# A fused attention and gated convolution kernel: a new written-out order of the same operations, with the 64-row score products in fewer runs

## The chip, the cores and the metric

The kernel runs on one core of one Trainium2 chip. A core has TensorE (PE, matrix products, with its weight loads listed as PEld), VectorE (DVE), ScalarE (ACT), GpSimd (POOL) and SyncE (SP). The engines run on their own and wait for each other through semaphores. The metric is the device time of one execution in microseconds (us), as a median over runs.

## What is computed

The inputs are q, k and v (4 batches, 8 heads, 768 positions, head size 64), a projection, a filter and an output matrix. In short:

```python
scores = q @ k^T / 8 - slope[h] * dist        # kept: the last 96 positions, and the first 8 ("global") ones
a = softmax(scores over the kept positions)
x = (a @ v), heads side by side               # 4 x 768 x 512
x1, x2, x3 = x @ w_proj, split in three
y = x1 * circular_convolution(x2, filter) * x3    # over the 768 positions, by Fourier transforms
out = y @ w_out
```

## The kernel before

Each batch goes through attention, gates and convolution. The work of all four batches is laid out as one list of operations, and one text says in which order every engine does them.

**The list.** `Plan.op` adds an operation: a cost per engine that may do it, what it reads and writes, and the PSUM banks that it takes (`acq`) or empties (`use`). An operation is a small group of instructions of one engine: eight banks of PSUM exist, an operation of TensorE takes one or two of them, and later operations on ACT or DVE copy the result out and so free them.

**The order.** The text `ORDER` holds one word for each operation: its number in the list, the engine that does it (P TensorE, A ACT, V DVE, G POOL, S SP) and, for an operation of TensorE, its banks. `119P45` is operation 119 on TensorE in banks 4 and 5, `120A` operation 120 on ACT. A word such as `i26b1` is 26 idle products into bank 1 (method `busy`, L302), which keep TensorE busy at the start. `Plan.schedule` only reads this text and checks it; the costs are not used in it. Each engine then does its own words in the order of the text, and waits where an operation needs data, or a bank that another engine has still to empty.

**The operations that matter here**, with their lines:

- *scores* (L680; in the first batch with added distance products, L671): q times k for two heads and two or three key tiles. Each product uses 64 of the 128 rows of TensorE, one head in the upper half and one in the lower. An operation has 4 or 6 such products (8 to 18 more with the distances), takes two banks, and is followed by one *exp* on ACT (L694), and but for the first batch by one mask product on DVE (L711). There are 48 score operations: 4 batches, 4 head pairs, 3 groups of key tiles. All other products of the kernel use 128 rows, but for a few of the setup.
- *values* (L729, L734), then *rc* and *xn* on DVE or ACT (the division, L758, L753 or L757), *trx* (a turn of x, L774) and its copy *xT*.
- *gate* (L843): x1 and x3, with their copies *x1* and *x3*, and *g* on DVE (L855).
- *butterfly* on DVE (L788 to L799), *proj* (L910), *fwd* (L614, and L593 for the filter), *prod* and *sums* on DVE, *inv* (L935, L938) with the copy *eo*, *mix* (L1018 to L1022), *half* and *y\*g* (L1041) on DVE, *out* (L962) with the copy *ot*, and the store.
- the turns of q and k (L627, L640) with the copies *qT* and *kT*.
- the filter's own transform in the first batch: sums on DVE (L556 to L572), `fwd` products, and copies.

**The loads.** POOL issues nearly all loads, one after the other, in the order of its words: keys (`kn`) and values (`vn`) by tile, q, blocks of the projection matrix (`w256`, `w0`, `w1280`, `w1024`, `w512`), the filter and `wo`. SP issues the first batch's q, the copies of the 8 global rows of k and v into the other tiles (`kglobal`, `vglobal`), and the stores. POOL also makes the tables of distances (operations 22 and 24) and the identity (operation 5).

Numbers used further on: 59, 61, 54 load key tiles 4, 6, 2 of the first batch; 157, 161, 163 to 169 are turns of k and scores of the first batch; 53 copies the global value rows to five tiles; 101, 106 are xn; 360 turns keys 0 and 1 of the second batch, and 404 is a copy xT; 249 is a product of the filter's transform; 283 is a proj, 400 a values, 410 a gate; 588 and 614 turn keys of the third batch; 973 is the last inv of the last batch, 994 to 1002 are its mix, half and y\*g steps, 1015 its last y\*g, and 1003, 1006, 1009, 1016, 1019, 1022 its last six out.

Of the kernel before, what the change touches and what calls it, by code (L numbers as in the profile page):

```python
# [16 lines left out]
P = 128  # L17
# [28 lines left out]
106V 4V 117P23 118A 167P01 168A 165P67 166A 163P45 164A 99P23 100V 101V 215P0 216A 76A 107P1 108V 130P67 131V  # L46
132V 125P23 126V 127V 217V 218V 169P45 170A 73A 102P1 103A 220P6 360P7 488G 490S 272G 495G 133P2 134A 219A
221A 128P3 129V 176P45 177V 178V 361V 171P01 172V 150P3 152V 173V 222V 223V 140P2 142A 356P4 357A 179P5 180V
135P7 358P3 359A 224A 137A 174P2 175V 209V 226V 201V 202V 151P4 153A 154V 204V 371P01 365P23 366A 372A 145P5
147V 208V 203V 210V 211V 205V 206V 196P4 227P6 232A 146P7 148A 149V 234V 230V 235V 212V 207V 213V 236V 237V  # L50
225V 373V 214V 136P5 138A 198A 182P2 192P3 194A 368P01 369A 362P45 363A 197P7 199A 191P3 141P0 143A 228A 231A
193A 229A 233A 144V 238V 370V 195V 298P1 285P0 286A 281P7 282A 184A 386P6 387A 299A 498G 499G 294P0 295A 384P7
385V 239V 367V 139V 283P3 284A 186P6 188A 394P45 395A 397P01 398A 430P7 431V 289P2 290V 364V 181P3 309P6 310A
183A 432P7 433V 240V 396V 503G 504G 278G 489G 492G 485G 486G 502G 497G 487G 388P45 389A 391P01 392A 434P2 435V
390V 491S 505G 501G 496G 187P6 189A 296P7 297A 379P45 380V 381V 436P23 437A 374P01 375V 399V 376V 393V 720G
247P6 248A 439P45 440A 441V 438V 307P7 308A 287P2 288A 241P3 442P01 443A 405P45 406V 190V 407V 242V 382P6 383A
243P7 244A 302P2 303A 400P01 401V 402V 377P6 378V 444V 445P45 446A 447V 408P7 245P3 246A 300P2 301A 249P01
251A 409A 250V 403P6 404A 253P45 254A 255A 304V 292V 448P23 449V 450A 185V 453P01 454V 291V 455V 293V 252V
200V 311V 312V 722S 493S 729G 426P7 420P6 421P4 415P5 417A 422A 423A 411P0 413A 410P1 584P5 585A 456P6 457V
305V 660P4 661A 588P0 589V 306V 717G 713G 735G 716G 718S 494S 714G 313P2 314A 317P3 451P5 452A 412A 318A 479V  # L60
478V 425P6 614P2 615A 727G 734G 506G 726G 280G 732G 662P0 719S 721S 464P4 466A 428A 427A 586P1 587V 414V 612P5
613V 481V 480V 725G 508G 724G 658P3 730G 500G 715G 728G 731G 733G 723G 507G 736G 321P2 322A 663A 323P4 324A
327P1 328V 429V 482V 659V 424V 483V 474P7 476A 319P2 320A 469P0 471A 599P45 600A 590P67 591A 325P2 315P1 316A
326A 473P0 475V 484V 329V 330V 331V 522P3 523A 625P45 596P67 597A 598V 622P01 623A 624V 468P2 526P3 527A 470A
626A 509P6 510V 592V 332V 333V 524P7 525A 616P01 593P23 594A 617A 511P6 512V 601V 595V 336V 513P7 514A 664P45
665A 619P23 667P01 668A 620A 458P6 460V 477V 337V 459P7 461A 517P4 416P5 418A 518A 607P01 602P23 603V 608V
419V 604V 609V 621V 618V 334V 666V 335V 627V 515P7 516A 535P5 536A 530P6 531A 350P4 351A 537P5 812P7 813A
353P6 354A 673P23 674A 538A 670P01 671A 463P4 465A 528P7 529A 842P6 843V 628P23 629V 462V 630V 675V 672V 344P5
610P6 611A 345A 816P4 890P7 605P2 606A 817A 633P01 634V 635V 669V 520V 539V 519V 533V 472V 347P6 348A 631P5
886P3 636P2 637A 887A 632A 891A 341P4 676P01 677V 814P6 815A 342A 681P23 682V 540V 678V 532V 683V 467V 534V  # L70
521V 840P5 841A 644P7 888P6 889A 646A 648P4 650A 653P5 655A 679P0 680A 643P1 645V 847P67 848A 821P45 822A
684P2 547P0 548V 685V 823V 706V 849V 707V 649P3 651A 555P6 556A 549P7 550A 853P01 827P45 828A 898P23 899A
545P6 546A 854A 338P7 339V 708V 340S 349S 352S 355S 346S 343S 638P4 640A 551P5 552A 541P2 553P3 554V 709V 710V
711V 543P6 544A 542A 557V 558V 712V 559V 702P7 818P01 819A 850P45 851A 687P6 639P3 641A 689A 642V 900V 820V
560V 652V 561V 564V 754P2 755A 704A 741P4 742A 844P01 845A 846V 829V 824P23 825A 826V 565V 562V 901P67 902A
739P5 740A 737P4 738A 750P0 892P23 895P67 896A 893A 751A 686P1 688A 752P5 692P4 694A 753A 763P2 743P3 765P0
766A 835P67 836V 837V 563V 903V 697P4 654P1 656A 764A 767V 894V 852V 897V 745P0 746A 699A 744A 578P5 758P1
756P2 757A 759A 856P67 857V 647V 855V 696P4 698A 566P3 567A 579A 568S 580S 830P01 831V 832A 858V 768V 747V
691P4 693A 909P23 910V 761V 581P5 582A 861P67 862V 863A 911V 748V 904P01 905V 749V 906V 760V 575P4 701P2 833P3
834V 657V 912P5 859P6 860A 913A 569P7 838P0 839V 762V 703V 864P6 865A 570A 571S 583S 907P1 908A 934V 935V 936V  # L80
937V 695V 938V 939V 940V 773P3 572P5 573A 774A 769P0 781P6 775P1 777P5 783P7 784A 776A 771P2 772A 782A 778A
770A 867P3 872P7 874A 869A 779P2 780A 785V 786V 700V 787V 788V 690V 789V 790V 791V 792V 958P1 954P0 955A 576A
959A 577S 574S 945P5 946A 941P3 942A 915P0 943P2 944A 969P6 970A 956P1 957A 947P7 948A 882P3 949P2 950A 917A
951V 919P4 967P1 968V 952V 971V 953V 972V 962P5 960P2 961A 884A 877P6 871P7 873A 963A 965V 964V 705V 966V 793V
876P2 866P3 868A 879A 870V 881P7 986P5 990P3 973P0 974A 991A 987A 794P6 977P1 978A 979P0 980V 988P3 989A 975P5
976A 883A 981V 875V 885V 982V 929P1 992P3 993A 878A 795A 994V 995V 983V 984V 996V 997V 985V 796S 800P5 801A
797P0 798A 799S 802S 914P7 916A 918V 999V 998V 880V 1001V 1002V 1000V 803P5 804A 805S 925P6 809P7 810A 811S
# [110 lines left out]
class Fused:  # L198
# [459 lines left out]
    def scores(self, hp, gi, near=False):  # L658
        nc, g = self.nc, self.g
# [567 lines left out]
```

## Time and profile before

| what | value |
|---|---|
| median of 3 runs | 174.96 us (174.43 to 175.25) |
| profiled execution, first to last instruction (span) | 172.9 us |
| median less span | 2.06 us |
| PE from 30 to 150 us | busy all the time |
| first and last product | 1.20 and 168.46 us (end) |
| granted TensorE clock | 1.000 |

The profile is of one execution; its own time is its span and what lies around it, and the median of the runs is 2.06 us above the span. Busy times are the union of an engine's instructions. The products are pipelined: in a timeline, a product's listed length reaches past the start of the next one, so the distance from start to start tells what it costs. The chain of work that ended last is followed back from the last instruction to whatever released each step.

### The profile page before, as it was taken

The numbers are of one execution on the slowest core, as the hardware profiler recorded it, in microseconds if no ns is written. First come the engines' busy times: TensorE is split into PE (matmuls) and PEld (weight loads), VectorE is DVE, ScalarE is ACT, GpSimd is POOL, SyncE is SP. The second block draws the span as 40 slices with busy tenths as digits, with TensorE's granted clock in tenths as the row PEclk, the third lists the DMA queues.
The fourth block names the chain that finished last, engine by engine and source line by source line (L and its number), as shares of the span: only waits on it lengthen the run. The fifth ranks groups of instructions, "written<-read, shape, count | busy, mean of one in ns | idle before, by whom it ended". The sixth has DMA issues, their size and how long they took to land.

```text
span 172.9 us, 4486 instructions
## 1 busy us (share of the span) xinstructions
PE 166.8 (96%) x1732; PEld 106.1 (61%) x1732; DVE 158.4 (92%) x352; ACT 151.9 (88%) x305; POOL 75.8 (44%) x97
## 2 busy tenths in 40 slices
PE   7998999999999999999999999999999999999990
PEld 2374988655665668764657867645577755574530
DVE  6869969999999999999999999999989999989970
ACT  2999899999999999999999999999797897678821
POOL 7999998629989964999760000000000000000000
PEclk9999999999999999999999999999999999999999
DMA  4999999999999996999999000720030303003554
GB/s 86 188 198 166 168 171 177 207 184 153 154 161 145 153 148 50 126 147 175 152 151 57 4 0 4 272 91 0 4 121 6 121 2 121 4 0 151 213 205 161
DMA packets 91133, 20.74 MB, mean 120 GB/s; under 512 B 83864, under 2 KB 88040, under 8 KB 91112
## 3 DMA queue, kind: packets, MB, share of 16 engines
q0 software_dynamic: 80912, 12.14, 96.6%
q1 hardware_dynamic: 10200, 8.31, 15.3%
q8 instruction: 13, 0.21, 0.5%
q14 instruction: 8, 0.07, 0.1%
HBM read 25.84 MB, written 6.29 MB: 186 GB/s over the span
## 4 chain that ended last, share of the span: by engine, by line
PE 93%; DVE 4%; issue 0%; ACT 0%; ACTq 0%; DVEq 0%
PE bank L843 25%; PE bank L910 12%; PE bank L962 12%; PE bank L614 6%; PE bank L680 6%; PE bank L640 6%; PE bank L935 5%; PE bank L302 5%; PE bank L729 4%; PE bank L774 4%; PE bank L734 3%; PE bank L671 2%; PE bank L938 1%; DVE KT L306 1%; DVE vn L1097 1%; DVE vn L306 1%
## 5 line engine op out<-in xcount | busy, mean ns | idle before, releaser
L843 PE MATMUL bank<-xT,w 128*128 128x384 f16 x256 | 48.7, 326 | 0.0
L694 ACT ACTIVATE E<-bank 128x864 f16<-128x864 f32 x48 | 40.6, 902 | 1.3 <-PE bank L680 1.3
L843 PEld LDWEIGHTS <-w 128*128 128x128 f16 x256 | 23.4, 98 | 15.6 <-issue 0.7
L322 POOL DMA_DIRECT2D kn<-in_k_dram x28 | 25.7, 921 | 10.7 <-PE bank L640 4.3
L322 POOL DMA_DIRECT2D vn<-in_v_dram x28 | 25.6, 921 | 1.7 <-DMA wo<-in_moe_w_out_dram 1.1
L962 PE MATMUL bank<-wo,y 128*128 128x512 f16 x96 | 23.8, 379 | 0.0
L711 DVE TENSOR_TENSOR E<-E,mask 128x864 f16<-128x864 f16 x36 | 20.6, 600 | 0.0
L322 POOL DMA_DIRECT2D qn<-in_q_dram x18 | 16.3, 918 | 0.3 <-issue 0.2
L753 DVE TENSOR_TENSOR xn<-bank,rc 128x512 f16<-128x512 f32 (+1 forms) x21 | 16.1, 771 | 0.3
L853 ACT CAST g<-bank 128x384 f16<-128x384 f32 x32 | 15.4, 512 | 1.1 <-PE bank L843 0.9
L310 ACT ACTIVATE ot<-bank 128x512 f32<-128x512 f32 x20 | 11.9, 611 | 4.9 <-PE bank L962 4.9
L729 PE MATMUL bank<-vn,E 128*128 128x65 f16 x224 | 15.2, 193 | 0.0
L729 PEld LDWEIGHTS <-E 128*128 128x128 f16 x224 | 14.0, 97 | 1.8
L734 PE MATMUL bank<-vn,E 128*128 128x65 f16 x192 | 14.9, 193 | 0.0
L306 ACT CAST eo<-bank 128x384 f16<-128x384 f32 x28 | 12.7, 512 | 1.7 <-PE bank L938 0.9
L680 PE MATMUL bank<-QT,KT 64*128 64x216 f16 (+2 forms) x224 | 14.0, 241 | 0.0
L306 ACT CAST X<-bank 128x512 f16<-128x512 f32 x22 | 12.7, 613 | 1.3 <-PE bank L614 1.2
L962 PEld LDWEIGHTS <-y 128*128 128x128 f16 x96 | 8.8, 98 | 8.1
L310 ACT ACTIVATE ab<-bank 128x512 f16<-128x512 f32 x22 | 12.8, 619 | 1.1 <-PE bank L910 1.0
L310 ACT ACTIVATE x<-bank 128x384 f16<-128x384 f32 x26 | 13.1, 523 | 0.8 <-ACT g L853 0.4
L734 PEld LDWEIGHTS <-E 128*128 128x128 f16 x192 | 13.1, 97 | 0.7
L680 PEld LDWEIGHTS <-KT 64*128 64x128 f16 x224 | 8.5, 94 | 6.6 <-issue 5.0
(144 smaller groups left out, 369.3 us busy)
## 6 DMA issues: line engine op xcount, KB each, us to landing
out_dram<-ot SPq DMA_DIRECT2D x24, 256.0 KB
kn<-in_k_dram POOLq DMA_DIRECT2D x28, 120.0 KB, 6.3
vn<-in_v_dram POOLq DMA_DIRECT2D x28, 120.0 KB, 6.4
qn<-in_q_dram POOLq DMA_DIRECT2D x18, 128.0 KB, 6.5
ot<-in_q_dram SPq DMA_DIRECT2D x6, 256.0 KB
w<-in_moe_w_proj_dram POOLq DMA_DIRECT2D x4, 256.0 KB, 7.3
g<-in_moe_filter_fft_dram POOLq DMA_DIRECT2D x1, 768.0 KB, 11.0
w<-in_moe_w_proj_dram POOLq DMA_DIRECT2D x1, 512.0 KB, 12.7
```

The costliest lines, as they stand in the source:

```text
L306: {"A": nc.scalar.copy, "V": nc.vector.tensor_copy, "G": nc.gpsimd.tensor_copy}[e](out, in_)
L310: self.nc.scalar.mul(out, in_, c)
L322: return self.g.op(eng, 0.57 + 0.00035 * nbytes[0] if eng == "G" else 0.5, lambda _: e.dma_start(dst, src), w=w, r=r, nbytes=nbytes, name= ...
L680: nc.tensor.matmul(bs[hh].f32()[:, off:off + w], self.KT[hs, hp, P * m:P * m + P], self.QT[hs, hp, KL * m:KL * m + w], start=(off == 0 and ...
L694: g.op("A", act(864), lambda _: nc.scalar.activation(eo, bs[0].two()[:, :, 0:432].rearrange("p h (m w) -> p h m w", m=2), Act.Exp, scale=s ...
L711: g.op("V", dve(864, 2), lambda _: nc.vector.tensor_mul(eo, eo, mk), r=[("mask", 2 * hp), ("mask", 2 * hp + 1)], w=[("E", hp, gi)], name=" ...
L729: nc.tensor.matmul(o[:, n, hh], ef[:, at:at + P], vt[:, t, 2 * hp + hh, 0:D + 1], start=first, stop=(t == 0), skip_group_check=True)
L734: nc.tensor.matmul(o[:, n, hh], ef[:, at:at + P], vt[:, t - 1, 2 * hp + hh, 0:D + 1], start=False, stop=True, skip_group_check=True)
L753: nc.vector.tensor_mul(to, o[:, :, :, 0:D], rc.to_broadcast([P, 2, 2 * nt, D]))
L843: nc.tensor.matmul(bk.f32()[:, 0:h], self.w[:, c, o + P * j:o + P * j + P], self.xT[:, c, h * s:h * s + h], start=(c == 0), stop=(c == 3))
L910: nc.tensor.matmul(bk.f32(), src[:, c], w[:, c, DM:2 * DM], start=(c == 0), stop=(c == 3))
L962: nc.tensor.matmul(bk.f32(), y[:, c, P * t:P * t + P], self.wo[:, c, :], start=(c == 0), stop=(c == 3))
```

## The change

`ORDER` is replaced by another order of the same operations: other sequences on every engine, other banks, and 56 operations that may be done by ACT or DVE on the other one of the two. The score operations stand in 19 runs on TensorE where they stood in 23. One idle product more is issued (26, 3 and 4 of them for 26, 2, 3 and 1). Two cost figures in the list change as well. The diff, cut to the parts that are spoken of:

```diff
 ORDER = """
-0V 8V 31V 11V 7V 12V 1V 10V 9V 17S 50S 15S 16S 48S 49S 58S 18G 5G 39A 35A 42A 43A 45A 41A 6A 47A 37A 32A 2A
-38A 36A 33A 46A 51A 19G 22G 23V 28A 40A 44A 26V 55G 24G 71V 72A 77A 34A 79A 52V 25V 61G 54G 59G 60G i26b1 80P0
-86P1 87V 81V 29V 259G 20G 21G 57G 67G 56G 62G 3G i2b3 89P2 90V 27V 30V 88V 53V 13V 261S 260G 64G 63G 65G 257G
-256G 258G 68G 66G 70G 69G 82P3 83A 84P4 85A 74A i3b1 109P5 110A 75A 115P3 116V i1b0 91P67 92A 93P01 94A 113P2
-114V 269G 270G 267G 268G 273G 263G 95P45 96A 78A 161P6 111P7 112V 157P3 158V 162V 14V 97P01 98A 119P45 120A
-123P23 124A 121P67 122A 159P0 160V 262S 265S 264S 275G 274G 276G 279G 277G 266G 271G 155P1 156V 104P45 105V
...
-920P5 922A 931A 806P0 807A 927A 921A 1014V 1012V 923V 1013V 808S 924P5 926A 928V 1006P7 1007A 1008S 930P6 932A
-933V 1015V 1009P4 1010A 1011S 1003P5 1004V 1005S 1022P4 1023V 1024S 1016P7 1017V 1018S 1019P6 1020A 1021S
+0V 17S 31V 15S 22G 16S 5G 35A 18G 7V 48S 6A 50S 32A i26b7 80P0 8V 11V 39A 84P1 23V 10V 24G 25A 19G 28A 49S
+i3b7 86P2 36A 47A 54G 55G 30V 26A 46A 40A 45A 3G 42A 58S 61G 20G 82P3 60G 71V 33A i4b7 89P4 44A 13V 37A 81A
+29V 41A 27V 109P0 72A 43A 85V 34A 83A 21G 59G 79A 87V 56G 88V 90V 9V 77A 4V 12V 95P45 91P23 111P1 57G 113P6
+110A 112V 96A 38A 64G 115P7 116V 63G 97P45 93P01 259G 114V 78A 92A 62G 121P67 51V 258G 98A 119P23 94A 155P4
+52V 123P01 14V 122A 159P5 120A 104P67 257G 157P2 124A 161P3 261S 158A 260G 156V 160V 105V 75A 99P45 162V
+117P01 106V 100V 53V 118A 256G 269G 169P23 170A 270G 167P67 67G 125P01 101V 168A 74A 262S 163P45 126V 165P23
...
+990P0 986P3 869A 568S 885V 920P7 870V 574S 991V 977P0 916V 798A 976A 973P1 799S 987A 794P4 978A 974A 994V 980V
+800P6 995V 795A 801A 996V 577S 981V 924P4 919P1 802S 997V 803P6 807A 926A 796S 930P0 804A 982V 998V 921A 983V
+1001V 984V 808S 985V 805S 1002V 999V 932A 809P4 918V 810A 1000V 929P6 922A 1014V 931A 1012V 1003P0 1009P1
+1006P6 923V 1010A 928V 933V 1013V 1015V 1022P1 1007V 1019P7 1011S 1023V 1004A 1005S 1016P6 1008S 1017A
+1020V 1024S 1021S 1018S
 """
...
-        g.op("P", 0.65 if near else 0.28, run, acq=bs, r=[("QT", t) for t in qt] + [
+        g.op("P", 0.56 if near else (0.19 if len(m0) == 2 else 0.2), run, acq=bs, r=[("QT", t) for t in qt] + [
...
-        g.op("P", 0.06 * 2 * len(ts), run, acq=[b], r=[("xn", j, c), "ident"], name="trx")
+        g.op("P", 0.0558 * 2 * len(ts), run, acq=[b], r=[("xn", j, c), "ident"], name="trx")
```

TensorE's runs of score operations, counted in the whole text: 6 of one operation, 11 of two, 4 of three and 2 of four before; 1 of one, 8 of two, 9 of three and 1 of four after.

More of the change, by code (lines that the diff above doesn't have):

```diff
@@ L50 @@
[L50 to L54, printed above, removed]
@@ new lines @@
+143A 206V 138A 182P3 184A 186P2 189A 373V 385V 435V 370V 207V 367V 388P67 139V 213V 389A 391P45 392A 149V
+394P01 285P3 430P6 432P7 272G 286A 144V 181P4 395A 214V 283P3 188A 433V 266G 499G 491S 183V 390V 505G 393V
+265S 226V 234V 396V 490S 235V 236V 486G 191P7 431A 485G 284A 193A 439P45 277G 445P01 446A 442P23 287P6 237V
+443A 278G 298P7 504G 294P0 440A 397P23 447V 436P45 295A 238V 299A 281P1 437A 489G 239V 296P7 282A 398A 196P4
+379P01 297A 380V 240V 289P5 374P23 302P7 198A 288A 381V 492G 375V 303A 498G 399V 376V 245P4 290A 400P01 497G
@@ new lines @@
+780A 566P3 777P5 695V 690V 913A 570A 876P2 567A 934V 773P3 935V 936V 872P0 778A 937V 938V 781P5 782A 774A
+958P4 939V 769P5 940V 772A 941P3 776A 770A 959A 881P7 956P1 785V 874A 786V 945P0 877P4 787V 957A 879A 878V
+960P2 942A 883A 882P1 788V 961A 954P4 962P7 943P5 789V 792V 955A 925P4 571S 967P2 963A 946A 790V 944A 791V
+969P0 970A 866P5 867P7 949P0 968A 947P2 965V 964V 884A 580S 927A 950A 966V 948A 915P4 349S 971V 972V 871P0
+583S 988P1 576A 979P6 793V 917A 880V 873V 975P4 992P0 797P2 989A 952V 875V 914P1 993A 868A 806P5 951V 953V
```

68 lines of the change are left out of this document (31 added, 37 removed).

## The prediction

> **What bounds the kernel now.** I read the page's busy time first, then the chain that ended last, then the sums of busy time by stage, and last TensorE's timeline, start by start. From the page:
>
> ```profile
> PE 166.8 (96%) x1732; PEld 106.1 (61%) x1732; DVE 158.4 (92%) x352; ACT 151.9 (88%) x305; POOL 75.8 (44%) x97
> ...
> PE 93%; DVE 4%; issue 0%; ACT 0%; ACTq 0%; DVEq 0%
> ```
>
> and from the busy time by stage (length, then PE, weight loads, DVE, ACT, POOL):
>
> ```profile
> 13.00:30.00 17.00, 16.52 (x318) 13.13 (x318) 14.46 (x31) 15.69 (x22) 16.44 (x21) 1.00 2.10 170
> 30.00:45.00 15.00, 15.00 (x127) 9.11 (x126) 14.93 (x36) 14.56 (x29) 9.70 (x12) 1.00 1.85 179
> 45.00:60.00 15.00, 15.00 (x183) 9.14 (x181) 14.88 (x34) 14.98 (x27) 14.32 (x17) 1.00 2.31 152
> ```
>
> TensorE carries the end nearly alone and never pauses after 30 us; DVE is hardly less full (14.93 of 15). So nothing can be won by waiting less after 30 us: only shorter TensorE work, the start, or the tail can win, and any wait on DVE that the new order creates is a loss. The same sums also show that both evacuating engines have almost no reserve in these stages. The tail is taut too: the last output operation starts at 167.43, and the y*g that the last three output operations wait for ends at 165.64, 0.07 us ahead of the first of them.
>
> Where TensorE's time goes beside its products is seen in its timeline (start, length with the pipeline's tail, line; start to start is what counts):
>
> ```profile
> 75.22 1.03 PE L910 MATMUL bank<-w,xo 128*128 128x512 f16 x4
> 76.18 0.73 PE L680 MATMUL bank<-QT,KT 64*128 64x216 f16 x12
> 76.84 0.82 PE L843 MATMUL bank<-xT,w 128*128 128x384 f16 x4
> ...
> 109.23 0.81 PE L843 MATMUL bank<-xT,w 128*128 128x384 f16 x4
> 109.98 0.54 PE L680 MATMUL bank<-QT,KT 64*128 64x216 f16 x8
> 110.46 1.47 PE L843 MATMUL bank<-xT,w 128*128 128x384 f16 x8
> ...
> 15.78 0.61 PE L627 MATMUL bank<-p,ot 128*128 128x128 f32 x4
> 16.82 0.38 PE L640 MATMUL bank<-ident,kn 128*128 128x128 f16 x4 [0.44 <-DVE KT L306]
> ```
>
> Four L910 products take 0.864 us start to start elsewhere; ahead of the 64-row L680 they take 76.18 - 75.22 = 0.96. Four L843 products, else 0.650, take 0.75. So going into 64-row products costs 0.10. Two score operations (x8) take 0.48, three (x12) 0.66: one more costs 0.185, and 0.48 - 2 x 0.185 = 0.11 is the way back. **A run of score products costs 0.20 us for its two ends, however long it is.** The last two lines show a stall: four L627 need 0.44, but the next starts 1.04 later, so 0.60 is lost; the product after it reads the keys that operation 59 loads, whose transfer was issued at 9.14 and whose last semaphore update comes at 15.9 (the row names DVE; the bank's copy had ended before).
>
> **The change, part by part.** The new cost figures at L688 and L775 sit in an argument that the written-out order never reads, so they move nothing: 0. All else is the order.
>
> *Runs of scores.* The 48 score operations form 23 runs on TensorE before (6 of one, 11 of two, 4 of three, 2 of four) and 19 after (1, 8, 9, 1). In the first batch there are five both times; later batches go from 18 to 14. 4 x 0.20 = **-0.80 us**, all on TensorE's path.
>
> The Trainium skill, "TensorEngine Tiling (Array Packing)", Key Properties, says that a change of tiling mode drains the array, and "TensorE: Matmul & The Clock Gate", Single matmul latency, gives a lone warm product 398 cycles beyond its columns, 0.166 us. Were every end of a run such a full drain, the eight ends saved would be an estimated -1.33; the rows show 0.10 each, and the sum goes by them.
>
> *Fillers.* Idle products (L302) are 26+2+3+1 = 32 before and 26+3+4 = 33 after. At 0.216 each: **+0.22**.
>
> *TensorE without any wait.* All other products are the same in number and shape, so TensorE's own line is 0.58 shorter. I call "wanted at" the place on this line, from the rows: gate 0.650, proj and out 0.864, inverse 0.330, values 0.030 a product, turns 0.056.
>
> *The start.* Before loses 0.23 at L671 (13.3), 0.60 at 16.1 and 0.14 at 43.6: 0.97 in all, and the new order need not lose these. It has its own. `161P` is ready at 20.1 on that line; DVE then does 162V 0.31, 106V 0.61, 100V 0.12, 53V 1.39, 101V 0.69: 23.2, and `163P`, wanted at 22.7, needs the bank that 101V frees: +0.5. 53V is the 8x2560 copy that lasts 1.47 us at 13.16 in the trace; before it stood where DVE had time.
>
> *The stage from 28 to 57 us.* After 360P, DVE has 62 operations up to `404V` in a row without a gap. By start-to-start distances of their rows: 11 masks of 0.52, 14 butterfly steps 5.2, the filter's sums 7.2, eight copies of q, k and xT 4.0 (0.3 to 0.6 each), four x1 1.9, six g 1.6, three xn 1.8, three rc 0.4, the twin table 0.6: 28.3. They start at 28.4 and end at 57.0 to 57.1; `249P`, wanted at 56.4, needs the bank that 404V frees. So +0.7; three more waits of the stage (283P, 400P, 410P) come out 0.6 to 0.8 late by the same addition, which is one debt and not four. In the old order this addition gives no wait later than 0.15, and TensorE lost nothing there. The two debts together lie between 0.7 (the first is worked off) and 1.2 (360P itself comes 0.5 late and DVE starts behind it). No row decides; I take **+1.0** in place of **-0.97**.
>
> *ACT* does 56 operations less or more than before in exchange with DVE; by their rows ACT has 6 us less (two of three scalings in many small pieces go to DVE), DVE 0.8 less. After 100 us the same additions give no wait late, so 0 there.
>
> *Transfers.* POOL's first key load moves behind the 1.9 us of IOTA and selects and the 0.56 of ident: issue at 3.8 instead of 1.30. w256 moves from 14.49 behind ten more loads, to 24; at 0.9 an issue and 5.0 to 7.2 from issue to landing it lands at 29.1 to 31.3 and is wanted at 30.6 (+0.5 from the start). Others stand alike: w1280 30.3 to 32.5 for 31.9, the filter 44.4 to 46.5 for 45.8, and the copy of the global value rows, issued when the values' first load lands (45.2 to 46.7) and 5.9 long in the trace of before, 51.1 to 52.6 for 50.6. With the 0.5 to 1.0 that TensorE is already late, the near ends cost 0, the far ends up to 1.3. I take 0: the loads stay one queue in which the landings follow each other at 0.86, the row that they are nearest to.
>
> *Tail.* From 994V to 1015V DVE has 23 instructions, 8.75 us by start-to-start distances; TensorE's rows from 973P to 1022P give 9.0. 0, and up to +1.4 if they didn't overlap. The last three copies and issues stay as they are.
>
> **Sum:** -0.80 + 0.22 - 0.97 + 1.0 = -0.55. The profiled span of 172.9 becomes 172.35; the median of 174.96 is 2.06 above the span, so 174.4.
>
> **Rivals.**
> *The debts don't come* (say DVE gains what the sums round up). Then -0.80 + 0.22 - 0.97 + 0 to 0.5: 173.4 to 173.9. For it: the same additions were 0.1 too strict in the old order. Against: two places with fresh sums, each several times that.
> *The transfers decide, slower.* If loads land at the far ends, TensorE waits for w256, for the global rows and through DVE for the filter: +1.3 on 174.4, and +0.5 more where the keys for 588P and 614P (0.4 and 0.5 ahead even by the near ends) come late: 175.7 to 176.2. It decides from landings about 1.5 us behind the near ends. For it: in the old order every landing is some 2 us later than the near ends. Against: TensorE is itself late by then.
> *Banks.* Nine runs of three hold six of eight banks while ACT needs 3 x 0.77 us for their exps, so the product behind the run waits for a bank. If each run lost 0.2, 9 x 0.2 = 1.8 takes more than the gain: 176.2. Against: the next products take the two free banks and those of copies on DVE; by the rows ACT frees the first bank 0.9 after the run began, the run itself takes 0.66. The Trainium skill, "TensorEngine Tiling (Array Packing)", Gotcha 1, warns of just this pressure; the old order's two runs of four held all eight banks in the first batch, without a stall at their ends.
>
> **How the numbers follow.** A difference of 0.5% (0.87 us) is about what a measurement of this kernel can tell. Forecast 0.45 (173.9 to 174.9; a third of it below 174.09, the bound of faster); no debts 0.27; transfers 0.20 (two thirds above 175.83); banks 0.08 (half above). Faster 0.15 + 0.27 = 0.42; slower 0.13 + 0.04 = 0.17; within 0.5% 0.41. The range reaches into the first two rivals: 173.3 to 175.9.
>
> **What would show it.** 19 runs, each with 0.10 ahead and 0.11 behind; a gap of TensorE of about 0.5 near 22.7 released by DVE xn, and gaps that add to 0.5 to 0.7 between 37 and 64 released by DVE copies; no gap after 100. Gaps released by a DMA, or by POOL's queue, would mean the second rival; gaps at the product behind three scores, released by ACT's exps, the third. A stall behind ACT anywhere after 100 us would make the whole working wrong.

## The result, and the profile after

The new order is slower by a third of a per cent: 175.27 us (median of 20 runs, 174.61 to 175.9) against 174.75 for the kernel before (20 runs beside it, 174.2 to 175.25). The ratio is 1.0034, 95% interval 1.0022 to 1.0046, so about 0.5 us where 0.55 us less was forecast. (The forecast's 174.4 stands on the 174.96 of the first three runs.) The profiled execution lasted 175.35 us, its span 173.6; the last product ends at 169.05 instead of 168.46.

From the page after (busy times, then the chain that ended last, by engine and by line):

```profile
PE 167.1 (96%) x1733; PEld 106.7 (61%) x1733; DVE 158.1 (91%) x348; ACT 149.9 (86%) x291; POOL 76.0 (44%) x97
...
PE 62%; DMA 17%; POOL 13%; issue 3%; DVE 3%; ACT 0%; POOLq 0%; DVEq 0%
PE bank L844 18%; PE bank L963 11%; PE bank L911 9%; DMA g<-in_moe_filter_fft_dram 7%; DMA vn<-in_v_dram 6%; POOL kn L323 6%; PE bank L936 5%; PE bank L615 5%; DMA w<-in_moe_w_proj_dram 4%; PE bank L681 3%; POOL vn L323 3%; PE bank L641 3%; PE bank L730 3%; PE bank L775 2%; PE bank L735 2%
```

The busy times hardly differ. The chain does: before it was TensorE for 93%, now DMA and POOL, which issues the loads, hold 30% of it. Which transfer it was has still to be found: the view infers the links of the chain, and one of them is wrong, as is seen below. (All lines of the code are one further down after than before.) The busy time by stage, in the columns of before:

```profile
13.00:30.00 17.00, 16.54 (x337) 14.41 (x336) 14.38 (x34) 16.22 (x26) 17.00 (x21) 1.00 2.13 152
30.00:45.00 15.00, 15.00 (x131) 9.13 (x129) 14.90 (x38) 14.81 (x25) 10.46 (x12) 1.00 1.71 184
45.00:60.00 15.00, 14.79 (x167) 8.56 (x166) 14.28 (x31) 14.58 (x28) 12.76 (x15) 1.00 2.37 155
```

In the last of them PE falls from 15.00 to 14.79 and DVE from 14.88 to 14.28: both now wait more. The busy PE still hides part of this, since a product's listed length reaches into a wait; start to start tells more. From TensorE's timeline after:

```profile
22.48 0.35 PE L681 MATMUL bank<-QT,KT 64*128 64x216 f16 x6
23.24 0.19 PE L730 MATMUL bank<-vn,E 128*128 128x65 f16 x1 [0.40 <-DVE vn L307]
...
75.39 0.73 PE L681 MATMUL bank<-QT,KT 64*128 64x216 f16 x12
76.06 0.82 PE L844 MATMUL bank<-xT,w 128*128 128x384 f16 x4
```

The first two lines are the wait that was forecast at the start: 125P stands 0.51 us behind its due time because 53V, the long copy of first value rows, ends at 23.18. The last two are a run of three scores: 0.67 start to start for 3 x 0.185 + 0.11, as before.

I then compared each operation of TensorE with the line that the prediction draws for "TensorE without any wait". That line is 0.59 us shorter after (166.25 for 166.84). The slip against it at the end is 1.44 us before and 2.62 after: +1.18. The sum, -0.59 + 1.18 = +0.59, is the difference of the two last products. The slip of after comes in these steps: 0.21 from the fillers (PE's clock rose one filler later), 0.13 at 95P, 0.08 at 123P, 0.16 at 157P, 0.51 at 125P, 0.19 at two changes of mode for small products that before has too, 0.15 at 434P, 0.13 in small drifts, 0.27 at 379P, 0.28 at 400P, 0.06 at 249P, 0.25 at 410P (65.65 us), and 0.23 in all the rest. (They add to 2.65 by rounding.) Before 66 us everything is lost, and nothing behind it that before does not lose as well.

The chain of work, in order of time, shows what stands behind 400P (start, length, what):

```profile
33.99 11.72 DMA g<-in_moe_filter_fft_dram
45.75 0.55 issue
46.30 0.90 POOL kn L323
47.20 1.78 POOL qn L323 x2
48.98 0.92 POOL vn L323
49.90 4.78 DMA vn<-in_v_dram
54.70 0.19 PE bank L730
```

A filter load that takes 11.7 us to land, loads behind it, and then something of `vn` that lands just ahead of 400P. The name needs care: the view names the newest load on a semaphore that 400P waits for, and 400P does not read those rows (the load that it needs on that semaphore landed at 49.02). Its first product also waits for the semaphore of the second copy of the global value rows (265S), which fills last. So what the view hangs ahead of 49.90 is not 400P's path. Both copies are in SP's queue (start, length of the issue; the row between them is 491S, a copy of keys for the third batch):

```profile
46.52 0.69 SPq L323 DMA_DIRECT2D vn<-vn  x1
47.38 0.69 SPq L323 DMA_DIRECT2D kn<-kn  x1
48.12 0.69 SPq L323 DMA_DIRECT2D vn<-vn  x1
```

The semaphore of the first is full at 52.26, 379P starts at 52.39; that of the second at 54.56, 400P starts at 54.70. Before, they were issued at 44.09 and 44.83, landed at 49.98 and 50.73, and 400P did not start until 56.53. So the new order wants these rows 1.8 us earlier (2.7 earlier on the line without waits: 52.6 for 55.3) and gets them 3.8 us later. The first copy is issued as soon as the load that it reads (263) has landed, at 46.46, and the second 1.6 us later. That load stands right behind the filter in POOL's queue. The filter, issued at 25.43 and landed at 36.40 before, is issued at 33.99 and lands at 45.71, because the rows of the second batch's earlier scores stand ahead of it in the queue.

The late filter by itself holds nothing in this kernel. It lands at 45.71, and DVE, which has no pause there, comes to its first sum only at 46.61, behind two masks and the twin table:

```profile
45.44 1.12 DVE L712 TENSOR_TENSOR E<-E,mask 128x864 f16<-128x864 f16 x2
46.47 0.22 DVE L434 TENSOR_SCALAR fwd<-fwd 128x256 f16<-128x256 f16 x1
46.61 0.95 DVE L557 TENSOR_TENSOR pp<-g 128x1536 f16<-128x1536 f16 x1
```

DVE's own list is close behind the copy, though: 400P also takes the banks that 381V, a division on DVE, frees, and 381V ends at 54.42, 0.14 us ahead of the copy's landing.

### The profile page after: what moved, and what is told of

Its sections match the earlier page's. It is cut to its first block, busy times and chain, and to the rows that moved or that the text cites. A ratio compares the mean times of both kernels' runs of the same rounds, so it can differ in the third digit from the quotient of the medians.

```text
span 173.6 us, 4455 instructions
## 1 busy us (share of the span) xinstructions
PE 167.1 (96%) x1733; PEld 106.7 (61%) x1733; DVE 158.1 (91%) x348; ACT 149.9 (86%) x291; POOL 76.0 (44%) x97
## 3 DMA queue, kind: packets, MB, share of 16 engines
HBM read 25.84 MB, written 6.29 MB: 185 GB/s over the span
## 4 chain that ended last, share of the span: by engine, by line
PE 62%; DMA 17%; POOL 13%; issue 3%; DVE 3%; ACT 0%; POOLq 0%; DVEq 0%
PE bank L844 18%; PE bank L963 11%; PE bank L911 9%; DMA g<-in_moe_filter_fft_dram 7%; DMA vn<-in_v_dram 6%; POOL kn L323 6%; PE bank L936 5%; PE bank L615 5%; DMA w<-in_moe_w_proj_dram 4%; PE bank L681 3%; POOL vn L323 3%; PE bank L641 3%; PE bank L730 3%; PE bank L775 2%; PE bank L735 2%
## 5 line engine op out<-in xcount | busy, mean ns | idle before, releaser
L754 DVE TENSOR_TENSOR xn<-bank,rc 128x512 f16<-128x512 f32 (+1 forms) x23 | 17.7, 775 | 0.4
L311 ACT ACTIVATE ot<-bank 128x512 f32<-128x512 f32 x21 | 12.6, 623 | 6.0 <-issue 3.5
L730 PE MATMUL bank<-vn,E 128*128 128x65 f16 x224 | 15.6, 193 | 0.6 <-DVE vn L307 0.4
L735 PE MATMUL bank<-vn,E 128*128 128x65 f16 x192 | 15.3, 193 | 0.0
L307 ACT CAST eo<-bank 128x384 f16<-128x384 f32 x26 | 11.9, 509 | 3.6 <-PE bank L939 3.4
L307 ACT CAST X<-bank 128x512 f16<-128x512 f32 x24 | 13.8, 609 | 1.1 <-PE bank L615 1.1
L311 ACT ACTIVATE ab<-bank 128x512 f16<-128x512 f32 x23 | 13.8, 620 | 0.9 <-PE bank L911 0.8
L735 PEld LDWEIGHTS <-E 128*128 128x128 f16 x192 | 13.2, 97 | 0.9 <-issue 0.4
L681 PE MATMUL bank<-QT,KT 64*128 64x216 f16 (+2 forms) x224 | 13.5, 241 | 0.0
L311 ACT ACTIVATE x<-bank 128x384 f16<-128x384 f32 x23 | 11.8, 520 | 0.2 <-ACT E L695 0.2
## 6 DMA issues: line engine op xcount, KB each, us to landing
g<-in_moe_filter_fft_dram POOLq DMA_DIRECT2D x1, 768.0 KB, 11.7
```

Of the source, the lines that this page charges most:

```text
L307: {"A": nc.scalar.copy, "V": nc.vector.tensor_copy, "G": nc.gpsimd.tensor_copy}[e](out, in_)
L311: self.nc.scalar.mul(out, in_, c)
L681: nc.tensor.matmul(bs[hh].f32()[:, off:off + w], self.KT[hs, hp, P * m:P * m + P], self.QT[hs, hp, KL * m:KL * m + w], start=(off == 0 and ...
L730: nc.tensor.matmul(o[:, n, hh], ef[:, at:at + P], vt[:, t, 2 * hp + hh, 0:D + 1], start=first, stop=(t == 0), skip_group_check=True)
L735: nc.tensor.matmul(o[:, n, hh], ef[:, at:at + P], vt[:, t - 1, 2 * hp + hh, 0:D + 1], start=False, stop=True, skip_group_check=True)
L754: nc.vector.tensor_mul(to, o[:, :, :, 0:D], rc.to_broadcast([P, 2, 2 * nt, D]))
```

## The experiments

Each ran beside the kernel before on the same chip, on five chips in all (174.68 to 174.75 us for before), so compare ratios first. The ratio need not be the quotient of the two medians (masks_out: 1.0045, medians 1.0027). `400P` and `rest` are of one profiled execution each: the start of 400P, and from there to the start of the last operation of TensorE.

| kernel | us | ratio to before, 95% | 400P | rest |
|---|---|---|---|---|
| after | 175.27 | 1.0034 (1.0022 to 1.0046) | 54.70 | 113.32 |
| start_repaired | 175.24 | 1.0032 (1.0016 to 1.0048) | 54.22 | 113.42 |
| copies_repaired | 175.43 | 1.0041 (1.0023 to 1.0060) | 54.31 | 113.35 |
| both_repaired | 175.37 | 1.0034 (1.0009 to 1.0060) | 54.70 | 113.35 |
| both_filler | 175.10 | 1.0017 (0.9999 to 1.0035) | 53.94 | 113.41 |
| start_repaired_less_loads | 174.26 | 0.9984 (0.9967 to 1.0002) | 53.49 | 113.34 |
| less_loads | 173.98 | 0.9973 (0.9951 to 0.9995) | 54.18 | 113.34 |
| masks_out | 175.15 | 1.0045 (1.0025 to 1.0066) | 55.04 | 113.35 |
| masks_out_copies_early | 175.08 | 1.0026 (1.0011 to 1.0042) | 54.05 | 113.73 |
| late_waits_moved | 175.40 | 1.0048 (1.0029 to 1.0068) | 53.79 | 114.37 |
| values_first | 175.65 | 1.0045 (1.0024 to 1.0065) | 53.19 | 115.00 |
| values_first_start_kept | 175.63 | 1.0050 (1.0032 to 1.0068) | 53.97 | 114.82 |
| filter_early | 176.68 | 1.0108 (1.0087 to 1.0128) | 56.49 | 113.34 |
| mark_128 | 180.85 | 1.0355 (1.0326 to 1.0383) | 56.77 | 116.79 |
| mark_64 | 175.63 | 1.0053 (1.0029 to 1.0076) | 54.32 | 113.89 |
| before_ones_moved | 174.69 | 0.9995 (0.9981 to 1.0009) | | |
| before_loads_moved | 174.70 | 0.9990 (0.9975 to 1.0006) | | |
| before_start_and_loads | 175.81 | 1.0058 (1.0038 to 1.0078) | | |
| before_then_after | 179.12 | 1.0245 (1.0223 to 1.0268) | | |

Theory at first: the new order's waits, at the start and at 28 to 66 us, ate the gain of the runs. Rivals: the grouping itself costs (banks, ACT); the load order costs.

### What a run of scores costs: mark_128 and mark_64

```diff
         def run(_):
             off = 0
+            half = slice(0, 128)          # mark_64: slice(0, 64)
+            nc.tensor.matmul(bs[0].f32()[:, 0:16], self.idle[half, 0:P], self.idle[half, 0:16],
+                             start=True, stop=True, skip_group_check=True)
```

> The order of after with one more product ahead of each of the 48 score operations: 128 rows, 16 columns wide, into the bank that the score product then overwrites. It makes every score operation a run of 64-row products of its own: 48 runs in place of 19. Theory (0.10 us to go into 64-row products and 0.11 us back): 29 runs x 0.20 = 5.9 us more than the same product in 64 rows, besides the price of the small products themselves. Rival (a change of mode costs nothing that isn't hidden, and the 0.20 us came of something else at these places): within 0.5 us of the same product in 64 rows.

> The same product ahead of each score operation, with 64 rows in place of 128: the runs stay 19. Theory: 48 products of 16 columns at 0.03 to 0.07 us each, 1.5 to 3.4 us more than after, and 5.9 us less than with 128 rows. Rival: as with 128 rows, within 0.5 us.

The two differ by 180.85 - 175.63 = 5.22 us, 0.18 for each of 29 runs more. From TensorE's timelines, first with 128 rows, then with 64:

```profile
77.67 0.18 PE L667 MATMUL bank<-idle 128*128 128x16 f16 x1
77.79 0.36 PE L684 MATMUL bank<-QT,KT 64*128 64x216 f16 x4
78.08 0.18 PE L667 MATMUL bank<-idle 128*128 128x16 f16 x1
```

```profile
75.08 0.45 PE L684 MATMUL bank<-QT,KT 64*128 64x216 f16 x5
75.30 0.17 PE L667 MATMUL bank<-idle 64*128 64x16 f16 x1
75.32 0.39 PE L684 MATMUL bank<-QT,KT 64*128 64x216 f16 x4
```

The small product and the score after it come round every 0.41 us with 128 rows and every 0.22 with 64: 0.19 for the two changes of mode. Behind 400P, where after has 24 score operations in 9 runs, the 15 runs more cost 2.90 us in the two profiles, 0.19 each. The price of a run is right, and so the first rival, that the grouping gains nothing, falls. A miss on the side: 48 small products in 64 rows cost 0.36 us in all by the medians (24 of them, behind 400P, 0.57 in the profiles), not 1.5 to 3.4. The Trainium skill, "TensorEngine Tiling (Array Packing)", Key Properties, has the drain at a change of mode; these runs put 0.18 to 0.20 us on a pair of changes.

### Mending the waits that the trace names

start_repaired (two DVE operations), copies_repaired (a load and two copies), both_repaired, both_filler:

```diff
-... 29V 41A 27V 109P0 ... 155P4 52V 123P01 14V 122A ... 106V 100V 53V 118A ...
+... 29V 41A 27V 14V 109P0 ... 155P4 52V 53V 123P01 122A ... 106V 100V 118A ...
```

```diff
-... 274G ... 275G ... 70G ... 263G 488G ... 264S ... 491S ... 265S ...
+... 263G 274G ... 275G ... 70G ... 488G ... 264S 265S 491S ...
```

> The order of after with two DVE operations moved earlier: 14V (fills of ones, 1.55 us) from 18.1 us to the idle stretch just before 85V at 9.8 us, and 53V (copy of first value rows, 1.4 us) to just behind 52V. Nothing else is changed. Theory (waits that the new order makes ate the gain of the score runs): the wait of 0.51 us ahead of 125P at 22.7 to 23.2 us goes, as do part of the 0.16 and 0.13 at 157P and 95P; 0.3 to 0.6 us less than after, so a ratio to before of 1.000 to 1.002 in place of 1.0034. Rival (the wait only moves, since the loads or ACT's exps are as late): the same as after within 0.15 us, ratio 1.0025 to 1.004.

> The order of after with the loads and copies of the second batch's global value rows moved earlier: 263G ahead of 274G, 275G and the filter in POOL's queue, and 264S and 265S ahead of 491S in SP's. Theory (transfers made the second part of the loss): 264 and 265 land by about 49 us in place of 52.3 and 54.6, the waits of 0.27 us at 379P and 0.28 us at 400P go, and the filter lands some 0.9 us later, which delays DVE's first sum of the filter by under 0.5 us; 0.3 to 0.55 us less than after, ratio to before 1.000 to 1.002. Rival (DVE's debt in the same stage is as late as the copies, so its values wait for the same instant): less than 0.15 us gained, and the gaps at 52 to 55 us are then released by DVE; ratio 1.0025 to 1.004.

> Both edits of the two kernels before this one in the list, together. Theory: the two gains add, 0.7 to 1.1 us less than after, which is 0.2 to 0.6 us below before (ratio 0.9965 to 0.999), since the score runs' gain of 0.6 us (after 0.2 us for one filler more) is then no longer eaten. Rival (the grouped order costs more in itself, by PSUM banks or cold clock, than the waits that the trace names): not below before, ratio 1.000 to 1.003.

> Both edits and the third group of filler products cut from 4 to 3, so that fillers number 32 as in before. By the row of a cold or warm filler (0.43 or 0.22 us each) 0.2 to 0.4 us less than with both edits alone, if PE isn't then waiting for what follows the fillers (89P4, which needs a load of keys); 0 if it is. Ratio to before 0.994 to 0.998 by the theory; if the third group's end is set by the load, the same as with both edits alone.

No gain from any of the first three; both_filler is 0.27 below both_repaired, within their intervals. Yet the waits named did go. In start_repaired 125P has no wait any more and 434P starts at 38.60 instead of 39.51 (0.25 of it is there ahead of 95P); then 379P waits 0.30 and 400P 0.67 for the same two copies (265S issued at 47.68, full at 54.08, 400P at 54.22). In copies_repaired the copies are there by 47.7, and 400P starts at 54.31 right behind 381V, which ends at 54.26. DVE did not wait for the filter there: that landed at 46.44, and DVE came to it at 46.86. So it is DVE's own list that is late, as the rival said. In both_repaired DVE comes to the filter sooner, the filter lands at 47.21, and 400P starts where it did in after, at 54.70. From the waits of both_repaired between 44 and 58 us:

```profile
DVE pp L555 <- DMA g<-in_moe_filter_fft_dram: 1.5, 1, 1.5
```

**What is mended ahead of 400P is taken back at 400P**, all of it in both_repaired, about half in start_repaired (0.91 us earlier at 434P, 0.48 at 400P). From there on the kernels with after's order need 113.3 to 113.4 us, as the table's last column shows (113.73 in masks_out_copies_early).

PE's clock gives a head start without any edit, but not one that can be followed here. In both_repaired it rose at 4.15 us, in after at 6.71, and 80P started 1.27 us earlier; at 95P 0.25 of that is left, since 14V, moved ahead on DVE, lets 95P start at 13.2 us in every kernel that has it there.

### The load queue: less work, and another order

start_repaired_less_loads and less_loads leave out five loads ahead of the filter:

```diff
     def load_rows(self, what, dst, src, b, t):
         lo, hi = self.K0[t], self.K0[t] + KL
+        if what == ("kn",) and b == 1 and t > 1:
+            self.loads += 1
+            self.g.op("G", 0.0, lambda _: None, w=[what + (t,)], nbytes=(0, 1), name="none")
+            return
```

> The kernel with the start repaired, and five loads of the second batch's key rows (269, 270, 276, 274, 275; all stand ahead of the filter in POOL's queue) left out, so that the second batch is computed with key rows of the first in their place; no other instruction is changed. Theory A (the waits of 0.30 us at 379P and 0.67 us at 400P, which stayed when the start was repaired, are the queue of loads: filter and global value rows come too late): the filter lands at 41 to 42 us in place of 45.3, DVE's sums of it and the copies of the value rows are done earlier, and both waits go: 0.7 to 1.0 us less than with the start repaired alone, ratio 0.9975 to 0.9995. Theory B (DVE has more to do up to there than it has time for, whenever the filter lands): the waits stay within 0.3 us, ratio 1.002 to 1.003.

> The order of after, unchanged, with the same five loads of key rows left out (the second batch is computed with key rows of the first). Together with the kernel that had the start repaired as well (174.26 us) it prices the start by itself. Theory (two groups of waits, and while the queue of loads holds the second, repairing the first is worth nothing): 0.4 to 0.7 us less than after from the second group, 174.6 to 174.9 us, and the start's repair is worth 0.4 to 0.7 us once the loads are out. Rival (only the loads count): 174.2 to 174.4 us, as with the start repaired.

Both are some 1.0 to 1.3 us faster than their counterparts by the medians (0.8 to 1.1 by the ratios). In less_loads the filter lands at 42.7, the copies at 46.79 and 49.74. The chain that ended last, by engine, of less_loads:

```profile
PE 85%; ACT 6%; DVE 4%; issue 3%; DVEq 0%
```

No DMA and no POOL is left in it. So theory A holds: 379P waits no more, and 400P still waits for 381V, but only 0.13 us (0.28 in start_repaired_less_loads). It is the copies that count in this and not the filter, which lands 3.0 us earlier than in after while DVE comes to it 0.10 earlier, at 46.51.

What the start is worth with the loads out stays open. By the medians it is nothing: less_loads, with every wait of after's start still in it (0.97 us by 23 us in its profile), is no slower than the one without, as its rival said. By the two profiles it is 0.69 us, as I had expected: with the start repaired 125P starts at 22.29 for 23.13, 400P at 53.49 for 54.18, and the last product ends as much earlier. But that profile of less_loads is one of its slower executions (174.82), with a clock that rose late, at 6.61. Its median gained more (1.29) than this execution shows at its last product (0.5); that an early rise, which after loses at 400P, now reaches the end would explain the rest, and it is argued, not shown.

With 0.27% below before (interval 0.05 to 0.49%), less_loads suggests that the shorter TensorE line can come through. It also leaves out five loads that before has, and no kernel here has before's order without them, so how much of this is the order's is not shown.

filter_early moves the filter's load instead of leaving others out:

```diff
-... 267G 268G 273G ... 69G ... 274G ... 275G ... 70G ... 263G ...
+... 70G 267G 268G 273G ... 69G ... 274G ... 275G ... 263G ...
```

> The order of after with the filter's load moved ahead of 267G, six loads earlier in POOL's queue. Theory (the queue is full, and the grouped scores of the second batch want their rows ahead of it, so the place of the filter can't be mended by itself): the filter lands at 39 to 40 us, the six loads behind it some 3.5 us later than now, and PE waits for them: 1 to 2.5 us at 384P, 285P and 432P, less up to 0.5 us that the later waits give back: ratio 1.006 to 1.015. Rival (the loads have slack that the new order doesn't use): faster than after, ratio 0.999 to 1.002.

As expected: the filter lands at 39.3, and TensorE waits some 2.4 us at 384P, ahead of its first product and within it, for q rows that land at 40.1 and 40.9. The waits from 36 to 46 us (engine, line, released by: us in total, times, longest):

```profile
PE bank L639 <- DMA qn<-in_q_dram: 2.1, 2, 1.6
```

The queue has no slack to give for this move: what the filter goes ahead of is late. And it gains nothing by the filter, since DVE comes to its first sum only at 48.60, more than 9 us behind the landing.

### The queue, or DVE's list behind it

late_waits_moved, values_first and values_first_start_kept keep all work and let DVE and 400P go round the filter:

```diff
-... 226V 234V 396V ... 447V ... 379P01 297A 380V 240V ... 381V ... 245P4 290A 400P01 ... 311V 612P3 ... 587V 450V ...
+... 396V 226V 234V ... 379P01 297A 380V ... 381V 240V ... 400P01 245P4 290A ... 447V ... 612P3 ... 587V 450V 311V ...
```

(values_first; late_waits_moved keeps 400P in its place and moves 240V ahead of 380V, and 185V, 190V, 305V and 311V behind 587V; values_first_start_kept has 14V behind 101V.)

> All work kept. The kernel with both repairs and 32 filler products, and six DVE operations moved: 396V into the idle stretch ahead of the filter's landing, 447V behind 402V, 240V ahead of 380V, and 185V, 190V, 305V and 311V, which are wanted only at 68 us, behind 587V. Theory (what is left there is DVE's list between the filter's landing at 46.7 us and 381V and 587V): 381V ends 0.5 to 0.8 us earlier and 587V by 1 us, so the waits at 400P (0.70) and 410P (0.32) shrink by 0.6 to 1.0 us: 174.1 to 174.5 us, ratio 0.996 to 0.999, faster than both kernels. Rival (copies and loads land as late as DVE's values): under 0.2 us, ratio 1.000 to 1.002.

> All work kept: the kernel with both repairs and 32 fillers, with 400P ahead of 245P on PE, 381V ahead of 240V, 396V ahead of 226V, 447V behind 402V, and 587V and 450V ahead of 311V on DVE. In every profile so far whose order from 400P on is after's, the last PE operation starts 113.35 us (113.3 to 113.4) behind the start of 400P. Theory (400P's start sets the time; DVE's list from the filter's landing to 381V sets 400P): 381V ends near 53.0 us, 400P starts at 53.0 to 53.4 us in place of 53.9, 410P waits less: 0.5 to 1.0 us less than with 32 fillers alone, 174.1 to 174.6 us, ratio 0.9965 to 0.9995. Rival (the copies of global value rows or another load hold 400P at 53.9): no gain, ratio 1.001 to 1.003.

> The same, but with 14V moved to just behind 101V (22.5 us) and not ahead of 85V, so that the start is free to profit where PE's clock rises early: it rose between 4.0 and 6.7 us in the profiles so far, and with 14V ahead of 85V the first score product starts at 13.2 us whichever it was. Theory: where 400P is mended the start counts: 0.1 to 0.4 us less than the kernel before this one in the list, ratio 0.995 to 0.999. Rival (nothing ahead of 400P counts): the same as that kernel within 0.15 us.

All three miss. In values_first 400P does start at 53.19, 0.75 us earlier than in both_filler; then 245P and 241P wait 0.11 each (245P for 240V), 249P 0.62 for 404V, 421P and 415P 0.70 for ACT, and the rest takes 115.0 instead of 113.4. From the waits of TensorE between 53 and 67 us:

```profile
PE bank L592 <- DVE xT L305: 0.5, 1, 0.5
PE bank L842 <- ACT g L852: 0.3, 1, 0.3
```

In late_waits_moved the operations put behind 587V make 450V and 322V late (0.69 at 593P, 0.33 at 323P). None of the three gained by moving work within DVE's list. That left open whether DVE's list itself or the transfers hold 400P, and the last two runs take DVE work away:

```diff
+        out = self.b == 1 and gi > 0
-        g.op("V", dve(864, 2), lambda _: nc.vector.tensor_mul(eo, eo, mk),
+        g.op("V", dve(864, 2), lambda _: None if out else nc.vector.tensor_mul(eo, eo, mk),
```

> The order of after with eight mask products of the second batch left out of DVE's list (390, 393, 396, 399, 438, 441, 444, 447, 0.57 us each, at 45 to 60 us), so that these exps stay unmasked; loads, copies, ACT and PE keep all. Theory (the copies of the global value rows, which landed at 54.56 us in after, and DVE's list hold 400P together): 400P gains under 0.3 us, 410P's wait of 0.25 us goes: 0.2 to 0.5 us less than after, ratio 1.0005 to 1.0025. Rival A (DVE's list alone holds): 0.9 to 1.4 us less, ratio 0.995 to 0.998. Rival B (DVE's list does not count): no change, 1.003 to 1.004.

> The same eight mask products left out of the kernel with the copies repaired (263G, 264S and 265S earlier). Theory: with copies and DVE's list both out of the way 400P starts at 52.8 to 53.4 us in place of 54.3 and 410P doesn't wait: 0.9 to 1.5 us less than with the copies repaired alone, ratio 0.9955 to 0.999, which is the gain of the grouped scores come through. Rival (the late filter's own sums or ACT hold 400P and what follows, whatever DVE is spared): under 0.4 us less, ratio 1.002 to 1.004.

With 4.6 us less to do, DVE has 381V ready at 53.80 in masks_out, after it has stood idle for 1.7 us ahead of 380V, and 400P starts at 55.04 all the same. Its waits from 44 to 70 us:

```profile
PE bank L731 <- DMA vn<-in_v_dram: 0.9, 1, 0.9
```

The second copy, issued at 48.24, is full at 54.91. With the copies early as well, the chain of masks_out_copies_early is

```profile
35.24 12.25 DMA g<-in_moe_filter_fft_dram
47.51 1.84 DVE pp L555 x2
49.37 0.69 DVE g L557
...
52.77 0.64 DVE g L571
53.41 0.60 DVE xn L753
54.01 0.04 issue
54.05 0.19 PE bank L729
```

DVE stood idle from 44.9 to 47.5 for the filter, did its seven sums without a mask between them, and had 381V done at 54.0, 6.5 us behind the landing. The median moved by 0.12 us in masks_out (its ratio the other way), and by 0.35 in masks_out_copies_early against copies_repaired, both within the intervals. So neither DVE's list nor the copies alone are the bound. **Three things stand within some 0.5 us of each other at 400P**: the second copy of the value rows (landed at 54.1 to 54.9 in after, start_repaired and masks_out), DVE's list up to 381V (54.42 in after, 54.26 in copies_repaired), and, once the copies are moved ahead, the filter with its sums (381V at 54.64 in both_repaired). Moving the copies ahead pushes the filter back by 0.7 to 1.9 us; of what was tried, only taking load out moved the copies without this. The theory, as far as it made DVE's debt the cause, falls: the copy is what holds 400P in after, start_repaired and masks_out. The rival of the load order stands, with DVE's list next behind it. Open is what the masks among the sums would cost if the copies came early and the filter no later; no kernel here has both.

### The order of before

```diff
-... 52V 25V 61G 54G ... 53V 13V 261S ...
+... 52V 25V 13V 61G 54G ... 53V 261S ...
```

> The order of before with one DVE operation moved: 13V (fills of ones, 1.55 us) from 15.0 us to just behind 25V, into DVE's idle stretch of 8.6 to 10.2 us. Theory (before's largest wait, 0.61 us ahead of 157P at 16.8 us, is the 1.55 us fill in front of 116V): the wait goes, 0.4 to 0.65 us less than before, ratio 0.9963 to 0.998, faster than both kernels. Rival (157P then waits for its load, which landed at 15.9 us, and the score products behind it for ACT's exps): a ratio of 0.998 to 1.0005.

```diff
-... 269G 270G 267G 268G 273G 263G ... 275G 274G 276G 279G 277G 266G 271G ...
+... 263G 269G 270G 267G 268G 273G ... 266G 275G 274G 276G 279G 277G 271G ...
```

> The order of before with two loads moved: 263G (second batch's first value rows, which the copies of global rows wait for) ahead of 269G, five loads earlier, and 266G ahead of 275G. Nothing else. Theory (before has the same bound behind it: 379P at 51.5 us stands within 1 us of these loads and copies, so that gains at its start are lost there): by itself no gain, ratio 0.998 to 1.001, since before's PE is not held by them; it shows in the next kernel.

```diff
-... 52V 25V 61G 54G 59G ... 29V ... 90V 27V 30V 88V 53V 13V 261S ... 158V 162V 14V ...
+... 52V 25V 29V 27V 30V 54G 61G 59G ... 90V 88V 53V 261S ... 158V 162V 13V 14V ...
```

> The same loads moved, and before's start mended: 54G ahead of 61G, 29V, 27V and 30V moved into DVE's idle stretch behind 25V, 13V (ones) from ahead of 116V to behind 162V. Theory: the waits of 0.23 us at 93P and 0.61 us at 157P go, and with the copies early nothing takes it back: 0.5 to 0.9 us less than before, ratio 0.995 to 0.9975, faster than both kernels. Rival (the start's gain is lost at another load or at ACT's exps, as when 13V alone was moved): ratio 0.9985 to 1.001.

```diff
-... 660P4 661A 588P0 589V 306V 717G 713G 735G ...
+... 660P4 661A 588P0 589V 306V 723G 614P3 615A ...
```

> The order of before up to 588P (66.4 us), and from there all operations that are left in the order of after: 22 runs of score products in place of 23, the later batches grouped as in after. Theory (the loss lies wholly ahead of 66 us): 0.2 us less than before, up to 0.3 us more where the two orders are joined; ratio 0.9985 to 1.001. Rival (grouping costs in the later batches too, by banks or exps): ratio 1.002 to 1.004.

before_ones_moved takes away the wait of 0.61 us at 157P and gains nothing: 113P now waits 0.54 for its key rows, which landed at 15.1 (14.4 in the profile of before), and 91P 0.55, within it, for 88V (0.23 in before). before_loads_moved gains nothing either, as expected by itself. before_start_and_loads is a miss of my own: 13V, put behind 162V, ends at 19.34 and delays 156V and 160V; 104P waits 0.22 for it and 0.41 more for a load of value rows, and 167P waits 1.29 for 156V. before_then_after tells little of what it was meant for: where the two orders are joined, 612P, 593P and 451P wait 3.3 us for copies and exps on ACT, and its slip grows from 1.6 to 5.6 between 58 and 80 us. From 80 us on it is after's order, and it slips 0.23 there.

Its first part, which is the order of before unchanged, tells something else. PE's clock rose earlier than in before's profile (5.27 us for 6.29) and 434P started 0.48 us earlier; then 379P waited for the second copy of the value rows, issued at 45.23 and full at 51.71, and started at 51.84, later than before's 51.51. Its waits of TensorE between 44 and 60 us:

```profile
PE bank L729 <- DMA vn<-vn: 0.6, 1, 0.6
```

So the old order, too, has these copies as a bound not far behind TensorE, and a better start was lost there in this execution. No kernel with all the work beat the kernel before by more than its interval.

## Why the prediction was wrong

- *Runs, -0.80, and filler, +0.22*: right. The line without waits is 0.59 shorter, and a run costs 0.18 to 0.20 by three readings.
- *The start, -0.97 for before's stalls and +0.5 for new ones*: the wait at 22.7 to 23.2 is there, 0.51, by 53V as said (at 125P instead of 163P). But the prediction missed three more waits (0.13 at 95P, 0.08 at 123P, 0.16 at 157P): 0.88 in all by 125P, where before loses 0.83 up to there. So the start brought nothing. Nor is the wait at 125P worth its length at the end: without it the median is 0.03 us lower. What before's stalls are worth is not shown, since others came in the place of the one that was taken away (0.05 us in the median).
- *The stage from 28 to 57 us, +0.7 as DVE's debt*: late by about that, 0.61 from 379P to 249P, but for another reason: 0.55 of it stands at 379P and 400P, each of which starts 0.13 to 0.14 us behind the landing of a copy. DVE's list is as long as was worked out: it runs from 29.69 to 58.51, and 0.33 and 0.25 us of that it waits at 380V and 404V, which leaves 28.2 for 28.3. (By its own terms, 28.4 and 28.3, the prediction's list ends at 56.7 and not at 57.0 to 57.1, so the +0.7 should have been +0.3.) With eight masks less for DVE nothing changed; with five loads less, 400P waits 0.13 to 0.28 for DVE, which is what was left of the debt there. 410P waits 0.25 in after and as much in less_loads, so the loads are not its cause.
- **The step that failed is the transfers: "With the 0.5 to 1.0 that TensorE is already late, the near ends cost 0, the far ends up to 1.3. I take 0".** The landings themselves came as worked out: the filter at 45.71 (44.4 to 46.5), the first copy at 52.26 (51.1 to 52.6). But the first copy, put at 0 with the others, made 379P wait 0.27, and the second, issued behind 491S and landed at 54.56 for a 400P wanted at 52.6, is not in the list at all: 400P waits 0.28 for it. With five loads less both waits go but for the 0.13 at 400P. Being late already did not pay for it: the transfers end at their own time, so the lateness of the start was absorbed in them and not added. The filter, which the list does name, cost nothing in after, as DVE came to it 0.90 us behind its landing.
- *ACT 0, tail 0*: right; the slip behind 66 us is 0.23.
- *Rivals.* "The transfers decide" (0.20) has the right mechanism and place. Its price, 175.7 to 176.2, added the far ends to a start that is late, where they overlap: 175.27. "No debts" is out by the waits above, and "banks" since no wait in after behind a run of three or four exceeds 0.16.

## What to carry to other kernels

Work out when each transfer ends from its own queue, then take the later of that and TensorE's own time; waits ahead of an instant that a transfer sets cost little or nothing, and mending them gains as little. An order that does one kind of work earlier also asks for its rows earlier, and in a full queue something else then comes later: follow what comes later through everything that hangs on it, and list every copy on the side queues. A view's name for a releaser is a guess where a wait has several semaphores: look at which one fills last. A wait that the trace names is worth its length only if nothing ends within that length behind it, which taking load out (not moving it) tells soonest.

## What was not expected of the hardware

- TensorE's clock rises at very different times: the fillers went from 427 to 216 ns each at 4.0 to 7.1 us, after 6 to 13 cold ones, over 20 profiled executions with the same first group of fillers. The Trainium skill, "TensorE: Matmul & The Clock Gate", What's actually happening, says that the window runs freely and that 6, 11 or 14 cold products are seen of one kernel; the counts here agree with that, but not with its spread of 500 ns either way, since here it is 3.1 us from end to end.
- Small copies within SBUF on SP's queue, 24 and 60 KB, take 5.7 and 6.4 us from issue to landing while POOL's queue is full, and 3.3 and 4.6 us with five loads left out. The Trainium skill, "DMA: Bandwidth & Descriptors", Queues, rings and completion order, says that an engine takes turns between queues packet by packet, which fits, if the copies run on engines that the loads use too; no view here splits a copy's time that far.
